# Warm-up matmuls on a preamble constant, an earlier gate for the wk load, and two matmuls ahead of Q, in a gated attention and feed-forward kernel

## The chip, the cores and the metric

The kernel runs on one core of a Trainium2 chip. The metric is the device time of one execution in microseconds (us). A core has five engines with instruction queues of their own: TensorE (PE, matrix products), VectorE (DVE), ScalarE (ACT), GpSimd (POOL) and SyncE (SP), which here issues transfers. Products of PE land in PSUM, from where VectorE and ScalarE copy them to SBUF, the working memory. Before the change the median of 8 runs is 267.02 us (266.33 to 267.93).

## The reference

```python
def _A_ref(x, wq, wk, wv, wo, beta):          # x: (1, 2048, 512), H = 32 heads of Dh = 16
    q, k, v = x @ wq, x @ wk, x @ wv          # as (B, H, N = 4 segments, L = 512, Dh)
    phi = lambda t: where(t > 0, t + 1, exp(t))
    M, z = 0, 0
    for s in range(4):
        p = softmax(qs @ ks.T * Dh ** -0.5 + causal_mask)
        a_dot = p @ vs
        a_mem = (phi(qs) @ M) / (phi(qs) @ z + 1e-6)
        outs.append(sigmoid(beta) * a_mem + (1 - sigmoid(beta)) * a_dot)
        M, z = M + phi(ks).T @ vs, z + phi(ks).sum(over the segment)
    return concat(outs) @ wo

def _B_ref(x, W_gate, W_up, W_down):          # F = 1792
    return (relu(x @ W_gate) * (x @ W_up)) @ W_down

g = sigmoid((A_x * gate_w).sum(-1))
return g * _A_ref(A_x, ...) + (1 - g) * _B_ref(A_x, ...)
```

## The kernel before

The sequence of 2048 rows is worked in four segments of 512. For each segment the kernel projects Q, K and V (matmuls of 128 x 128 against 512 columns, four to a result), forms the scores of 32 heads in 18 score products (`f`, L738, narrow matmuls of 32 rows), each followed by one exponential on ScalarE (L752, 1.9 us) and by causal masks on GpSimd (L760), and then the value products (`pv`, L849). Beside that run the gate and up products of the feed-forward part (`g` and `u`, 14 of each to a segment, L248), a ReLU on ScalarE, a product on VectorE, and the down and output products (`d` and `wo`). After each segment a state update (`mz`, L611) and reads of the state (`den`, `rec`) carry the memory M and z on. All dense matmuls are recorded at L248 by the helper `mm`; when the array is already laid out in column strips they are cut into four (L246).

The order of the work is not written by hand. The kernel records some 1350 operations with their engine, estimated cost, dependencies and buffers. A list scheduler (`Sched.run`) takes for each engine the operation that can start first, by keys, and emits all of them in that order. `MM` is the planned cost of a dense matmul, `SW` that of a change between PE's layouts (whole, rows, pairs, column strips); other costs stand in the calls of `op`. A change of a planned cost can thus change the order of all engines' instructions.

Four tiles G and one tile S in PSUM take PE's results. A G tile is used again only once its result has been copied out; S holds one score product at a time.

The start, which the change touches, goes as follows. The framework's preamble has GpSimd fill four small constant tiles, among them one of bfloat16 ones, and then releases all engines. `c_zero` has VectorE fill 128 x 128 ones in `zero`, a part of the output buffer `os` (L253). `c_dummy` (L291) runs 28 matmuls on `zero`, whose results nobody reads. `c_warm` (L263) runs one Exp on one column of `zero`, which loads ScalarE's table. SyncE and ScalarE each issue two quarters of the first segment's x, GpSimd issues wq in three pieces (L322). PE transposes x (`first_x`, L385) in groups of four matmuls, VectorE and ScalarE copy the transposes to xT (L393, L395), and PE forms Q for the first segment (L406) piece by piece of wq. K of the first segment follows, and needs wk.

The load of wk is tied to `o_wk0`, a memset of a single element of `wk_sb` on VectorE (L335). The planner puts it behind the first copy of xT. The transfer overwrites the element, so it has to wait for the memset, and SyncE, which issues in order, waits with wk and everything behind it: wv, gate_w, beta, and the pieces of W_gate and W_up.

Of the kernel before, what the change touches and what calls it, by code (L numbers as in the profile page):

```python
# [7 lines left out]
BF16 = mybir.dt.bfloat16  # L8
F32 = mybir.dt.float32
ACT = mybir.ActivationFunctionType  # L10
ALU = mybir.AluOpType

P = 128
# [12 lines left out]
VW = H * HP + 16  # L26
VSW = H // 2 * HP + 16

MM = 0.216
SW = 0.1  # L30
MG = 1.0


# [133 lines left out]
def kernel(  # L167
# [15 lines left out]
    nc = tc.nc  # L183
# [6 lines left out]
    def tl(name, shape, dt=BF16):  # L190
        return sb.tile(list(shape), dt, name=name)
# [11 lines left out]
    ident = tl("ident", [P, P])  # L203
    mcol = tl("mcol", [P, 1], F32)
    mcole = tl("mcole", [P, 1], F32)
    scratch = tl("scratch", [P, 1], F32)
    bdm = tl("bdm", [P, 8, DH], F32)
    mzacc = tl("mzacc", [P, NC, 2 * (DH + 1)], F32)
    M2 = [tl(f"M2_{i}", [P, NC, 8, DH]) for i in range(2)]
# [13 lines left out]
    Op_ = pool("O", 4, [P, 16, 2, DH])  # L223
    oTp = pool("oT", 8, [P, L])
    osp = rgp = pool("os", 4, [P, D])
    zero = osp.tiles[0]
    smp = pool("sm", 3, [P, 2, 16], F32)
    zg, zc, rcol, rp1, ngcol = (tl(n, [P, NT], F32) for n in ("zg", "zc", "rcol", "rp1", "ngcol"))
    R = [tl(f"R{s}", [P, 4, 4], F32) for s in range(NSEG)]
# [9 lines left out]
    op = sc.op  # L239
# [9 lines left out]
    ACTC = lambda n: 0.19 + 0.000833 * n  # L249


    def c_zero(e):
        nc.vector.memset(zero[:, 0:P], 1.0)  # L253
    o_zero = op("zero", {"DVE": 0.15}, c_zero, cls=0, key=-100)

    def c_ident(e):
        nc.gpsimd.memset(ident[:], 0.0)
# [2 lines left out]
    o_ident = op("ident", {"POOL": 0.6}, c_ident, cls=0, key=-100)  # L260

    def c_warm(e):
        nc.scalar.activation(scratch[:], zero[:, 0:1], ACT.Exp)  # L263
    o_warm = op("warm", {"ACT": 1.5}, c_warm, deps=[o_zero], cls=0, key=-100)

    def c_mcol(e):
# [20 lines left out]
    o_bdm = op("bdm", {"POOL": 1.5}, c_bdm, deps=[o_ident, o_vones], key=-10)  # L287

    def c_dummy(e):
        for _ in range(28):  # L290
            nc.tensor.matmul(g_dummy.t[:, 0:P], lhsT=zero[:, 0:P], rhs=zero[:, 0:P], start=True, stop=True)  # L291
    g_dummy = Buf(G)
    o_dummy = op("dummy", {"PE": 3.0}, c_dummy, deps=[o_zero], key=-1000, mode="D", alloc=[g_dummy])

# [18 lines left out]
    for i in range(2):  # L313
        for eng, q, h in (("SP", nc.sync, 0), ("ACT", nc.scalar, 1)):
            def f(e, i=i, q=q, h=h):
                q.dma_start(out=xn[0].t[:, 2 * h:2 * h + 2, 256 * i:256 * i + 256],
                            in_=x[256 * h:256 * h + 256, 256 * i:256 * i + 256].rearrange("(t p) d -> p t d", p=P))
# [14 lines left out]
        return load(name, f, P * tile_.shape[1] * (c1 - c0) * 2, key, eng=eng)  # L332

    lw["wk"] = loadw("wk", wk_sb, A_wk, 0, D, 1)
    o_wk0 = op("wk0", {"DVE": 0.08}, lambda e: nc.vector.memset(wk_sb[0:1, 0, 0:1], 0.0), key=-490, cls=0)  # L335
    lw["wk"].deps.append((o_wk0, None))
    lw["wv"] = loadw("wv", wv_sb, A_wv, 0, D, 1)

# [63 lines left out]
    first_x(1, None)  # L402
    for ci in range(NC):
        def f(e, ci=ci):
            for c in range(NC):
                nc.tensor.matmul(qS.t[:, c, :], lhsT=wq_sb[:, ci, c * P:(c + 1) * P], rhs=xT[0].t[:, ci, :],  # L406
                                 start=(ci == 0), stop=(ci == NC - 1))
        o_q0 = op(f"q0.{ci}", {"PE": 4 * MM * (1.5 if ci < 2 else 1)}, f,
                  deps=xc0[ci] + lwq[ci] + [(o_q0, 0.0) if ci else None],
                  key=-400 + ci, mode="D", alloc=[qS] + q0 if ci == 0 else [], uses=([] if ci == 0 else [qS]) + [xT[0]])  # L410
        if ci < 2:
            first_x(ci + 2, o_q0)
# [203 lines left out]
    def mz_deps(s):  # L616
        return [o_pKt[s, c] for c in range(NC)] + [o_v[s, t] for t in range(4)]
# [21 lines left out]
    def mz0():  # L639
        g = Buf(G)  # L640
        k = dkey(3)
        a = op("mz0", {"PE": 0.5}, lambda e: mz_mm(0, g), deps=mz_deps(0), key=k, mode="C", alloc=[g], uses=[pK[0], Vp[0]])
        mz_after(0, a, g, k)


# [74 lines left out]
    def unit(i):  # L720
        s, c = units[i]
        base = TA0 + (i // 2) * 2 * PU
        odd = i % 2
        FL = [[(c, 0, 0, 512)], [(c, 1, 0, 448), (c, 7, 448, 64)], [(c, 2, 0, 384), (c, 6, 384, 128)],
              [(c, 3, 0, 320), (c, 5, 320, 192)]]
        if not odd:
            FL.append([(c, 4, 0, 256), (c + 1, 4, 256, 256)])
        E, masks = {}, []
        for n, parts in enumerate(FL):
            sp, eb_ = Buf(Spool), Buf(Ep)  # L730
            kf = base + (n + 5 * odd) * 2 * PU / 9
            chunks = sorted({p[0] for p in parts})

            def f(e, parts=parts, sp=sp):
                for cc, kb, off, w in parts:
                    for j in range(4):
                        rows = slice(32 * j, 32 * j + 32)
                        nc.tensor.matmul(sp.t[:, j, off:off + w],  # L738
                                         lhsT=K2[s, cc].t[rows, kb, :, :].rearrange("p r k -> p (r k)"),
                                         rhs=QT[s, cc].t[rows, L - w:L], start=True, stop=True,  # L740
                                         tile_position=(32 * j, 0))
            a = op(f"f{s}{c}.{n}", {"PE": MM}, f,
                   deps=[o_q[s, cc] for cc in chunks] + [o for cc in chunks for o in o_k2[s, cc]] +
                   ([(fill_prev[0], 0.0)] if fill_prev[0] else []),
                   key=kf, mode="R", alloc=[sp], uses=[b_ for cc in chunks for b_ in (QT[s, cc], K2[s, cc])])
            fill_prev[0] = a
            if n == 1 and pending[0] is not None:
                rest(*pending[0], a)
                pending[0] = None

            def f(e, sp=sp, eb_=eb_):
                nc.scalar.activation(eb_.t[:], sp.t[:], ACT.Exp, scale=SCALE)  # L752
            b = op(f"e{s}{c}.{n}", {"ACT": 1.88}, f, deps=[a], key=kf, cls=0, alloc=[eb_], uses=[sp])
            offs = [p[2] for p in parts]

            def f(e, eb_=eb_, offs=offs):
                for off in offs:
                    for r in range(2):
                        v = eb_.t[64 * r:64 * r + 64, :, off:off + 64]
                        nc.gpsimd.affine_select(out=v, in_=v, compare_op=ALU.is_ge, fill=0.0, base=0,  # L760
                                                pattern=[[0, 4], [1, 64]], channel_multiplier=-1)
            m = op(f"m{s}{c}.{n}", {"POOL": 0.95 * len(parts)}, f, deps=[b], key=kf, uses=[eb_])
            for cc, kb, off, w in parts:
                if cc == c:
                    E[kb] = (eb_, off)
                else:
                    shared[s, cc] = (eb_, off, m)
            masks.append(m)
        if odd:
            E[4] = shared[s, c][0:2]  # L770
            masks.append(shared[s, c][2])
        pending[0] = (i, E, masks)
        if i == len(units) - 1:
            rest(i, E, masks, None)
# [4 lines left out]
    def dens(s, k0, org):  # L779
# [11 lines left out]
        rec_of[s, "den"] = rec_of[s, "mz"] = a  # L791
        if mds:
            gm = Buf(G)
            rec_of[s, "mz"] = am = op(f"mz{s}", {"PE": 0.5}, lambda e: mz_mm(s, gm), deps=[(a, 0.0)], key=k0 - 20, mode="C",
                                      alloc=[gm], uses=[pK[s], Vp[s]])
            gate_mz.append((s, am, gm, k0))
        T = Buf(Tp)
# [33 lines left out]
    def rest(i, E, masks, behind):  # L831
# [4 lines left out]
        def f(e):  # L836
            for kb in range(8):
                src, off = E[kb]
                w = L - 64 * kb
                for r in range(2):  # L840
                    rows = slice(64 * r, 64 * r + 64)
                    for j in range(4):
# [3 lines left out]
                        else:  # L846
# [1 line left out]
                            v = VS[s].t[rows, kb // 2, h * HP:h * HP + 32]  # L848
                        nc.tensor.matmul(gs[r].t[32 * j:32 * j + 32, L - w:L], lhsT=v, rhs=src.t[rows, j, off:off + w],  # L849
                                         start=(kb == 0), stop=(kb == 7), tile_position=(64 * r, 32 * j))  # L850
        a = op(f"pv{s}{c}", {"PE": 1.05}, f,
               deps=[(m, MG) for m in masks] + [o_v[s, t] for t in range(4)] + [o for t in range(4) for o in o_vs[s, t]] +
               ([(behind, 0.0)] if behind else []),
               key=k0 - 100, mode="P", alloc=gs, uses=list({id(v[0]): v[0] for v in E.values()}.values()) + [Vp[s], VS[s]])
# [170 lines left out]
```

The softmax here doesn't subtract the row's maximum and nothing guards it: scores larger than these inputs give would overflow.

## Time and profile before

| | us |
|---|---|
| median of 8 runs | 267.02 |
| profiled execution | 267.08 |
| its span, first to last instruction | 265.4 |
| PE busy | 260.5 (98%) |
| ScalarE busy | 194.1 (73%) |
| GpSimd busy | 191.3 (72%) |
| VectorE busy | 183.6 (69%) |
| wk, from issue to landing | 4.6 |

In a line of the timeline the first number is the start from the span's begin, the second the length, then follow engine, line of the kernel, operation, the tiles written and read, and the number of instructions that the line gathers. What stands in brackets is the engine's idle time just before, and what ended it. PEld is PE's weight load, SPq an issue of a transfer by SyncE. In a line of the chain of work, which is followed back from the last instruction, the time is that of a piece in which one engine went on without waiting. In the table of stretches the columns are the stretch, its length, the busy time of PE, PEld, DVE, ACT and POOL, PE's granted clock, the share of the DMA engines and GB/s. Matmuls overlap: the length of a group reaches to the modelled end of its last one, so distances are read from start to start.

### The profile page before, as it was taken

To read this page: it belongs to the slowest core of one execution; us is meant where nothing else is said; L and a number is where in the kernel's file an instruction comes from. 1 tells how busy PE (TensorE), PEld (TensorE's weight loads), DVE (VectorE), ACT (ScalarE), POOL (GpSimd) and SP (SyncE) were. 2 spreads that over 40 slices of the span, in tenths; PEclk is the share of its full clock that TensorE was granted. 3 is DMA by queue.
4 is the path that set the end of the run, shared out by engine and by line. 5 is a ranking of instruction groups with operands and counts; after the bars stand their busy time and mean duration, and the time that the engine had idled before them with its cause. 6 is when DMAs were issued, how large, how long until landed. Compare 5 with 4: busy or idle time off the path is not lost.

```text
span 265.4 us, 7084 instructions
## 1 busy us (share of the span) xinstructions
PE 260.5 (98%) x2844; PEld 115.0 (43%) x2844; DVE 183.6 (69%) x407; ACT 194.1 (73%) x189; POOL 191.3 (72%) x470
## 2 busy tenths in 40 slices
PE   8999999999999999999999999999999999999995
PEld 6434444444354434444444434344443444344444
DVE  1497888889975285998888837688985735566611
ACT  3598999899885558899896668898788566777010
POOL 8668888888559788798648988887878866537000
PEclk9999999999999999999999999999999999999999
DMA  5897990016310100000550010000000010000011
GB/s 161 248 266 198 337 268 15 4 40 69 111 26 1 42 20 22 0 2 2 117 110 16 21 42 20 4 2 0 2 0 4 0 42 23 20 2 0 2 41 40
DMA packets 27057, 15.54 MB, mean 59 GB/s; under 512 B 13584, under 2 KB 26896, under 8 KB 27024
## 3 DMA queue, kind: packets, MB, share of 16 engines
q1 hardware_dynamic: 26304, 14.30, 22.2%
q0 software_dynamic: 176, 0.52, 0.7%
q8 instruction: 22, 0.36, 0.6%
q10 hardware_dynamic: 544, 0.26, 0.3%
q14 instruction: 11, 0.09, 0.1%
HBM read 9.84 MB, written 2.10 MB: 45 GB/s over the span
## 4 chain that ended last, share of the span: by engine, by line
PE 96%; DMA 2%; DVE 0%; issue 0%; DVEq 0%
PE G L248 76%; PE S L738 9%; PE G L849 7%; PE G L246 3%; DMA wk_sb<-in_A_wk_dram 2%; PE G L291 1%; PE G L611 1%; PE G L785 0%; PE G L385 0%; DVE os L700 0%; DVE xT L393 0%; DVE os L253 0%; DVE mcole L268 0%; DVE wk_sb L335 0%; DVEq L700 0%
## 5 line engine op out<-in xcount | busy, mean ns | idle before, releaser
L752 ACT ACTIVATE E<-S 128x2048 bf16<-128x2048 f32 x72 | 135.1, 1876 | 34.5 <-PE S L738 32.1
L760 POOL TENSOR_SCALAR_AFFINE_SELECT E<-E 64x256 bf16<-64x256 bf16 x256 | 116.0, 453 | 38.1 <-ACT E L752 24.4
L248 PE MATMUL G<-xT,wu_sb 128*128 128x512 bf16 x218 | 58.3, 380 | 0.0
L248 PE MATMUL G<-xT,wg_sb 128*128 128x512 bf16 x218 | 57.9, 380 | 0.0
L663 DVE TENSOR_TENSOR hT<-G,os 128x512 bf16<-128x512 f32 x56 | 38.2, 684 | 20.2 <-ACT os L659 10.8
L248 PE MATMUL G<-wd_sb,hT 128*128 128x512 bf16 (+1 forms) x222 | 50.7, 366 | 0.0
L884 DVE STREAM_TRANSPOSE T<-G 128x512 f32<-128x512 f32 x44 | 30.3, 702 | 14.0 <-PE G L849 8.3
L659 ACT ACTIVATE os<-G 128x512 bf16<-128x512 f32 x56 | 32.7, 597 | 6.1 <-PE G L248 5.3
L248 PEld LDWEIGHTS <-wu_sb 128*128 128x128 bf16 x218 | 19.9, 98 | 24.8 <-issue 3.0
L248 PEld LDWEIGHTS <-wg_sb 128*128 128x128 bf16 x218 | 19.4, 98 | 24.6 <-issue 4.1
L248 PEld LDWEIGHTS <-hT 128*128 128x128 bf16 x222 | 20.3, 98 | 22.3 <-issue 2.6
L738 PE MATMUL S<-QT,K 32*128 32x192 bf16 (+7 forms) x512 | 28.5, 287 | 0.0
L738 PEld LDWEIGHTS <-K 32*128 32x128 bf16 x512 | 8.2, 92 | 30.3 <-issue 29.9
L700 DVE TENSOR_SCALAR os<-G,ngcol 128x512 bf16<-128x512 f32 (+1 forms) x10 | 7.0, 696 | 19.3 <-PE G L248 19.2
L849 PE MATMUL G<-E,Vp 64*32 64x128 bf16 (+7 forms) x512 | 19.0, 284 | 0.1
L849 PE MATMUL G<-E,VS 64*32 64x128 bf16 (+7 forms) x512 | 18.4, 284 | 0.0
L248 PE MATMUL G<-wo_sb,oT 128*128 128x512 bf16 (+1 forms) x68 | 17.6, 367 | 0.0
L597 POOL COPY VS<-Vp 64x256 bf16<-64x256 bf16 x32 | 13.3, 417 | 4.9 <-DVE Vp L515 3.5
L248 PE MATMUL G<-xT,wk_sb 128*128 128x512 bf16 x62 | 16.0, 380 | 0.5 <-DMA wk_sb<-in_A_wk_dram 0.5
L702 ACT ACTIVATE os<-G,ngcol 128x512 bf16<-128x512 f32 x7 | 4.8, 687 | 15.0 <-PE G L248 15.0
L904 DVE TENSOR_TENSOR O<-T,sm 128x256 bf16<-128x256 f32 x32 | 15.6, 516 | 0.3
L479 POOL COPY R<-rcol 32x4 f32<-32x4 f32 x64 | 13.5, 211 | 3.0
(98 smaller groups left out, 300.7 us busy)
## 6 DMA issues: line engine op xcount, KB each, us to landing
out_dram<-os SPq DMA_DIRECT2D x15, 128.0 KB, 1.7
wd_sb<-in_B_W_down_dram SPq DMA_DIRECT2D x1, 1792.0 KB, 12.6
xn<-in_A_x_dram SPq DMA_DIRECT2D x3, 512.0 KB, 4.7
wg_sb<-in_B_W_gate_dram SPq DMA_DIRECT2D x2, 512.0 KB, 5.9
wu_sb<-in_B_W_up_dram SPq DMA_DIRECT2D x2, 512.0 KB, 7.0
wg_sb<-in_B_W_gate_dram SPq DMA_DIRECT2D x3, 256.0 KB, 6.6
wu_sb<-in_B_W_up_dram SPq DMA_DIRECT2D x3, 256.0 KB, 6.9
wk_sb<-in_A_wk_dram SPq DMA_DIRECT2D x1, 512.0 KB, 4.6
```

Of the source, the lines that this page charges most:

```text
L246: nc.tensor.matmul(out_ap[q], lhsT=lhsT[:, q], rhs=rhs, start=start, stop=stop, tile_position=(0, 32 * j))
L248: nc.tensor.matmul(out_ap, lhsT=lhsT, rhs=rhs, start=start, stop=stop)
L479: nc.gpsimd.tensor_copy(R[s][32 * j:32 * j + 32, k, :], rcol[32 * k:32 * k + 32, cols])
L597: nc.gpsimd.tensor_copy(VS[s].t[64 * r:64 * r + 64, t, 0:H // 2 * HP].rearrange("p (h v) -> p h v", v=HP)[:, :, 0:DH], src[:, :, r, 0:DH])
L659: nc.scalar.activation(rg.t[:], g.t[:], ACT.Relu)
L663: nc.vector.tensor_tensor(h.t[:], u.t[:], rg.t[:], ALU.mult)
L738: nc.tensor.matmul(sp.t[:, j, off:off + w], lhsT=K2[s, cc].t[rows, kb, :, :].rearrange("p r k -> p (r k)"), rhs=QT[s, cc].t[rows, L - w:L] ...
L752: nc.scalar.activation(eb_.t[:], sp.t[:], ACT.Exp, scale=SCALE)
L760: nc.gpsimd.affine_select(out=v, in_=v, compare_op=ALU.is_ge, fill=0.0, base=0, pattern=[[0, 4], [1, 64]], channel_multiplier=-1)
L849: nc.tensor.matmul(gs[r].t[32 * j:32 * j + 32, L - w:L], lhsT=v, rhs=src.t[rows, j, off:off + w], start=(kb == 0), stop=(kb == 7), tile_po ...
L884: nc.vector.transpose(T.t[:].rearrange("p b e -> p (b e)"), g.t[:])
L904: nc.vector.tensor_tensor(O.t[:, :, r, :], T.t[:, :, 0:DH], sm.t[:, r, :, None].to_broadcast([P, 16, DH]), ALU.mult)
```

## The change

The ones tile and its memset go. Warm-up matmuls and the Exp read the preamble's constant of ones, broadcast along the columns. There are 31 warm-up matmuls instead of 28. The Exp writes its result into the first column of `wk_sb`, and the memset of `wk_sb` becomes an empty operation, so that the transfer of wk is ordered behind the Exp. The planner still sees `zero` and `wk0` with their former costs. Two matmuls of ones are put ahead of Q's first four, into S, which these overwrite. Beside that, planned costs are changed: `MM` 0.216 to 0.2159, `SW` 0.1 to 0.094, score products `MM` to 0.229, value products 1.05 to 1.015, state updates 0.5 to 0.56. With them the planner's order differs from near the first segment's end on.

```diff
-MM = 0.216
-SW = 0.1
+MM = 0.2159
+SW = 0.094
...
-    scratch = tl("scratch", [P, 1], F32)
...
-    zero = osp.tiles[0]
...
-    def c_zero(e):
-        nc.vector.memset(zero[:, 0:P], 1.0)
-    o_zero = op("zero", {"DVE": 0.15}, c_zero, cls=0, key=-100)
+    ones = nc.const_aps.tensor(1.0, [P, P], BF16)
+    o_zero = op("zero", {"DVE": 0.15}, lambda e: None, cls=0, key=-100)
...
     def c_warm(e):
-        nc.scalar.activation(scratch[:], zero[:, 0:1], ACT.Exp)
+        nc.scalar.activation(wk_sb[:, 0, 0:1], ones[:, 0:1], ACT.Exp)
...
     def c_dummy(e):
-        for _ in range(28):
-            nc.tensor.matmul(g_dummy.t[:, 0:P], lhsT=zero[:, 0:P], rhs=zero[:, 0:P], start=True, stop=True)
+        for _ in range(31):
+            nc.tensor.matmul(g_dummy.t[:, 0:P], lhsT=ones, rhs=ones, start=True, stop=True)
...
-    o_wk0 = op("wk0", {"DVE": 0.08}, lambda e: nc.vector.memset(wk_sb[0:1, 0, 0:1], 0.0), key=-490, cls=0)
+    o_wk0 = op("wk0", {"DVE": 0.08}, lambda e: None, key=-490, cls=0)
     lw["wk"].deps.append((o_wk0, None))
...
         def f(e, ci=ci):
+            if ci == 0:
+                for _ in range(2):
+                    nc.tensor.matmul(qS.t[:, 0, 0:P], lhsT=ones, rhs=ones, start=True, stop=True)
             for c in range(NC):
                 nc.tensor.matmul(qS.t[:, c, :], lhsT=wq_sb[:, ci, c * P:(c + 1) * P], rhs=xT[0].t[:, ci, :],
                                  start=(ci == 0), stop=(ci == NC - 1))
...
-        a = op("mz0", {"PE": 0.5}, lambda e: mz_mm(0, g), deps=mz_deps(0), key=k, mode="C", alloc=[g], uses=[pK[0], Vp[0]])
+        a = op("mz0", {"PE": 0.56}, lambda e: mz_mm(0, g), deps=mz_deps(0), key=k, mode="C", alloc=[g], uses=[pK[0], Vp[0]])
...
-            a = op(f"f{s}{c}.{n}", {"PE": MM}, f,
+            a = op(f"f{s}{c}.{n}", {"PE": 0.229}, f,
...
-            rec_of[s, "mz"] = am = op(f"mz{s}", {"PE": 0.5}, lambda e: mz_mm(s, gm), deps=[(a, 0.0)], key=k0 - 20, mode="C",
+            rec_of[s, "mz"] = am = op(f"mz{s}", {"PE": 0.56}, lambda e: mz_mm(s, gm), deps=[(a, 0.0)], key=k0 - 20, mode="C",
...
-        a = op(f"pv{s}{c}", {"PE": 1.05}, f,
+        a = op(f"pv{s}{c}", {"PE": 1.015}, f,
```

## The prediction

> **What bounds the kernel now.** I read the page's busy shares first, then its chain of waits.
>
> ```profile
> span 265.4 us, 7084 instructions
> ...
> PE 260.5 (98%) x2844; PEld 115.0 (43%) x2844; DVE 183.6 (69%) x407; ACT 194.1 (73%) x189; POOL 191.3 (72%) x470
> ...
> PE 96%; DMA 2%; DVE 0%; issue 0%; DVEq 0%
> ```
>
> TensorE (PE) is the chain for 96% of the span. So only three things can move the time: work on PE, gaps between its matmuls, and the tail after the last one. The one DMA in the chain is wk, 2% of the span. Next I read the timeline of the first 16 us.
>
> ```profile
> 0.89 0.17 DVE L253 MEMSET os<- 128x128 bf16 x1 [0.89 <-PEq L1009]
> ...
> 1.12 3.17 PE L291 MATMUL G<-os 128*128 128x128 bf16 x28 [1.12 <-DVE mcole L268]
> ...
> 3.15 0.20 ACT L263 ACTIVATE scratch<-os 128x1 f32<-128x1 bf16 x1
> ...
> 4.08 1.06 PE L385 MATMUL G<-ident,xn 128*128 128x128 bf16 x8
> ...
> 5.19 1.23 PE L406 MATMUL S<-xT,wq_sb 128*128 128x512 bf16 x4
> 5.20 0.06 DVE L335 MEMSET wk_sb<- 1x1 bf16 x1
> 5.31 0.37 SPq L331 DMA_DIRECT2D wk_sb<-in_A_wk_dram  x1
> ...
> 9.93 2.76 PE L248 MATMUL G<-xT,wk_sb 128*128 128x512 bf16 x12 [0.47 <-DMA wk_sb<-in_A_wk_dram]
> ...
> 13.91 0.10 PEld L738 LDWEIGHTS <-K 32*128 32x128 bf16 x4 [0.42 <-DVE K L561]
> ```
>
> SyncE issues wk's transfer at 5.31, just behind VectorE's one-element memset of wk_sb, which ends at 5.26. PE wants wk when Q is through and waits for it until 9.93. The other gaps I looked for in a table of stretches:
>
> ```profile
> 9.46:9.93 0.47, 0.00 (x1) 0.01 (x1) 0.00 (x0) 0.44 (x1) 0.47 (x1) 1.00 1.09 383
> 9.93:13.92 3.99, 3.99 (x19) 1.68 (x21) 3.03 (x7) 2.99 (x6) 1.27 (x6) 1.00 0.85 218
> 13.92:44.90 30.98, 30.98 (x337) 12.98 (x336) 26.29 (x66) 28.16 (x32) 26.08 (x71) 1.00 0.93 225
> 44.90:46.40 1.50, 1.38 (x73) 0.84 (x66) 1.10 (x4) 1.50 (x2) 1.27 (x4) 1.00 0.00 0
> 46.40:262.00 215.60, 215.60 (x2367) 93.71 (x2366) 151.03 (x316) 157.94 (x145) 154.01 (x378) 1.00 0.11 26
> ```
>
> The second and third figures are the stretch's length and PE's busy time. From 9.93 to 262 PE is never idle but for 0.12 us near 45. There a value product (pv of segment 0, chunk 1) waits for GpSimd's masks, and takes 1.41 us from its first matmul to the next operation's, where its like takes 1.11: a stall of 0.30. So the kernel has two gaps worth a name: wk, and that 0.30.
>
> **The change, part by part.** The profiled execution took 267.08 us, 265.4 of them span and 1.68 around it. The median of the runs is 267.02, so the sum is made on the profiled one and carried over 0.06 lower.
>
> *wk.* The Exp that loads ScalarE's table now writes one column of wk_sb, and the transfer waits for that write instead of the memset. The row above ends at 3.35, and from VectorE's memset to SyncE's issue took 0.05, so wk is issued at about 3.40, 1.9 earlier. It took 4.57 from issue to landing (9.88), so with nothing else on the DMA engines it lands near 8.0. The wait of VectorE's memset for the first copy of xT goes with it. Behind wk on SyncE's queue stand wv, gate_w, beta and the first W_gate and W_up pieces. They wait for transfers that landed by 4.7, and move up too. Nothing of SyncE is held back, since it had nothing else to do between 1.77 and 5.31.
>
> What does PE get? Q's last matmul starts at 9.08 and the next at 9.93, where the usual distance is 0.216: 0.63 us. Not all of it is kept. The first score matmuls (13.92) need a K tile that VectorE finishes at 13.29, and VectorE and ScalarE work towards it from Q's end at 9.46 without regard to when wk comes: four Q evacuations, each behind the other, from 9.49 to 12.17, then the copies of K and the masks on it. The K tile is thus ready for PE at about 13.35, 0.57 before PE uses it. With wk early that product waits next, for 0.06. Gain 0.57.
>
> *Warm-up.* Without the memset PE waits only for the release at the start. VectorE went from its release (0.75) to its first instruction in 0.15; PE's release ends at 0.78, so I put its start at 0.92, between 0.85 and 1.0. The 28 matmuls stand 0.1067 apart, so 31 take 3.31, and the transposes begin at about 4.23, 0.15 later than now. The x they wait for landed at 3.88, so nothing but the warm-up holds them. The copies of xT shift by 0.15 with them, and so does Q's first matmul, to 5.33.
>
> Against this stands the clock. Its record rises to full at 5.65, 4.53 after PE's start; the 128-column matmuls stand 0.107 apart before and 0.056 after. Q's first four take 1.07 instead of 0.86, so 0.21 is lost to the slow clock. Were the rise tied to PE's start, it would come at 5.45 and Q would lose only 0.06: Q's end then stays where it is. Were it fixed in time, Q would lose 0.16 and end 0.10 late. I take 0, between −0.15 (transposes in part at full clock) and +0.10.
>
> The Trainium skill, page "TensorE: Matmul & The Clock Gate", section "Part 1: The HAM clock gate", says that the rise follows a free-running window of 3.4 us, so that it need not follow an earlier start, and varies by half a microsecond between runs. This trace shows one rise only, and cannot confirm it; by the rule, as my estimate, the warm-up would be worth anything from −0.25 to +0.25.
>
> *Fillers.* Two matmuls of 0.107 after the first eight transposes, 5.08 to 5.30, while PE waits for xT and wq until 5.33. They cost nothing while that wait covers them, and 0.21 if it were gone. They write a part of S that Q then overwrites.
>
> *wq beside wk.* wq's packets fill the DMA engines from 3.8 to 5.8. wk's first packet went out 0.9 after issue, so now it comes at about 4.3, in the middle of them. The three wq pieces landed at 5.08, 5.67 and 6.69 and are used at 5.19, 6.48 and 7.57. The last has 0.88 to spare. At best nothing changes; at worst all of wk's 512 KB goes first, at the 75 KB per 0.2 us that the trace shows, 1.4 us, and Q waits 0.5. The slack is nearer to a shared delay of half of that (0.7), so I take 0.
>
> The page "DMA: Bandwidth & Descriptors", section "Queues, rings and completion order", speaks against this: an engine takes turns between queues, packet by packet, so wk would slow wq. With turns even in bytes, my estimate from it is a delay of some 0.7 to 1.0 and a wait of at most 0.1.
>
> *The order.* New planner costs move PE's order from the 117th of its 584 operations on, near 50 us. Compared in the two builds: 72 score products, 16 value products, three state updates, 12 reads in both; 170 changes of tile layout before, 171 after; 34 dense matmuls cut into four column strips before, 12 after. Prices come from the chain:
>
> ```profile
> 14.31 2.70 PE G L248 x12
> 17.34 2.70 PE G L248 x12
> ...
> 78.13 2.60 PE G L246 x48
> ```
>
> Twelve dense matmuls take 12 times 0.216 = 2.59, so a score product with both its changes of layout is 3.03 − 2.59 = 0.44, of which its own matmuls take 0.33 and the changes 0.11. Strips (48 for 12) cost no more than whole matmuls: 0 to 0.2 over 22 of them. The one more change is +0.1. So the moved order is worth +0.1, and its real risk is new waits. The shortest distances that PE leaves others shrink in places: 1.42 us, three times, between a gate product and the next that uses its bank (1.52 once before). ReLU there takes 0.60 and the hand-overs some 0.25, so it holds while ScalarE comes at once; 1.39 held in the trace of before. I take no new wait, between 0 and +1.3. The 0.30 near 45 stays, as it lies before the reordering, or goes.
>
> Sum: −0.57 + 0 + 0 + 0.1 = −0.47; 267.02 − 0.47 is about 266.5. A difference of 0.2%, 0.53 us, is about what a measurement of this kernel can tell from none, so the forecast lies on that edge.
>
> **The rivals.** *A new wait in the moved order (slower).* A score exponential takes 1.88 on ScalarE. Where one starts just ahead of a ReLU that PE's bank waits for, the bank is free 0.25 + 1.88 + 0.60 = 2.7 after the product, and PE, which left 1.42, waits 1.3. The places are the gate products 3 and 7 of segment 2 and 0 of segment 3. One such place gives 267.02 − 0.47 + 1.3 = 267.85. It turns the sign once it costs more than 0.47 and counts as slower from 1.0. For it: ScalarE is 73% busy, and the 0.30 near 45 shows that plans are missed. Against it: in all three places the new order on ScalarE has the ReLU ahead of that exponential.
>
> *wq late behind wk (no difference).* Q waits up to 0.5 for its third piece, and what wk gave is gone: 267.0. It decides once that piece lands after 7.57. For it: DMA is full from 4 to 5.6. Against: 0.88 of slack.
>
> *Clock early and the stall gone (faster than forecast).* The rise comes before Q and the 0.30 near 45 goes: −0.15 − 0.30 more, 266.05. For it: PE starts 0.2 earlier and has no hole before Q. Against: nothing in the masks' order ahead of 45 changes.
>
> **How the numbers follow.** Forecast 0.52 (266.2 to 266.8), more gain 0.16, wq late 0.15, new wait 0.17. Of the forecast's half, 0.30 lies below the edge at 266.49 and 0.22 above it, as the Q of more runs than the profiled one may meet an earlier clock. So faster is 0.30 + 0.16 = 0.46, same 0.22 + 0.15 = 0.37, slower 0.17. The range reaches from 266.0, which takes in the case of more gain but for its end, to 267.6, which takes in wq late and the smaller new waits.
>
> **What would show it.** PE's first matmul near 0.9; wk issued near 3.40 and landed before 9.3; no PE gap ahead of the first K matmul; the first score matmuls near 13.35 instead of 13.92; the clock's rise at 5.45 or earlier; no new PE gap after 50. It would be wrong if wq's third piece landed after 7.57, if Q ended later than 9.5, or if PE waited for ScalarE or a bank in segments 1 to 3.

## The result: slower by half a percent, and the profile after

The changed kernel takes 268.40 us in the median of 11 runs (267.59 to 269.28), the one before 266.98 in the median of 32 (266.33 to 267.93). The ratio is 1.0055, with a 95% interval of 1.0042 to 1.0067: slower by 1.42 us. The forecast was 266.5, with a range that ended at 267.6, and mostly for faster. It was wrong in sign and size.

The profiled execution took 268.40, of which 266.7 are span and 1.7 lie around it. So in this pair of executions all of the loss lies in the span (265.4 before). The page, its first lines and its chain:

```profile
span 266.7 us, 6972 instructions
...
PE 261.1 (98%) x2783; PEld 115.5 (43%) x2783; DVE 180.6 (68%) x401; ACT 196.6 (74%) x193; POOL 190.3 (71%) x470
...
PE 95%; DMA 2%; POOL 1%; DVE 0%; issue 0%; POOLq 0%; DVEq 0%
PE G L246 77%; PE S L738 9%; PE G L849 7%; DMA wq_sb<-in_A_wq_dram 2%; PE G L244 1%; PE S L406 1%; PE G L611 1%; POOL wq_sb L319 0%; PE G L785 0%; DVE hT L663 0%; DVE os L700 0%; POOL ident L255 0%; POOL ident L254 0%; POOLq L255 0%; DVEq L700 0%
```

The changed kernel's file is two lines shorter ahead of the helper `mm`: its dense matmuls stand at L246, and those cut into column strips at L244. The shares hardly differ from those of before. What tells is the name of the one DMA in the chain: it was wk, and is now wq. The timeline of the first 16 us shows the place:

```profile
0.83 3.46 PE L288 MATMUL G<-const-bfloat16-1.0 128*128 128x128 bf16 x31 [0.83 <-PEq L1009]
...
3.15 0.20 ACT L260 ACTIVATE wk_sb<-const-bfloat16-1.0 128x1 bf16<-128x1 bf16 x1
3.38 0.37 SPq L328 DMA_DIRECT2D wk_sb<-in_A_wk_dram  x1
...
4.09 1.06 PE L382 MATMUL G<-ident,xn 128*128 128x128 bf16 x8
...
4.95 0.42 PE L404 MATMUL S<-const-bfloat16-1.0 128*128 128x128 bf16 x2
...
5.20 1.14 PE L406 MATMUL S<-xT,wq_sb 128*128 128x512 bf16 x4
...
9.15 1.90 PE L406 MATMUL S<-xT,wq_sb 128*128 128x512 bf16 x8 [1.50 <-DMA wq_sb<-in_A_wq_dram]
...
10.88 2.75 PE L246 MATMUL G<-xT,wk_sb 128*128 128x512 bf16 x12
...
14.94 0.10 PEld L738 LDWEIGHTS <-K 32*128 32x128 bf16 x4 [0.50 <-DVE K L561]
```

wk is let go at 3.38, as intended. But Q stops for 1.50 us ahead of its third part, for wq's third piece, and starts it at 9.15 (7.57 before). That piece, issued at 3.18 in both kernels, landed at 6.69 before and at 9.10 now. K then follows without a gap, but from 10.88 (9.93 before), and the first score matmuls start at 14.94 (13.92 before), 1.02 later. wk itself landed at 9.86, against 9.88 before: 1.92 earlier on its way, and not a bit earlier there. From the first score matmuls to the end the two executions differ by 0.29; that is no more than the kernel before differs from itself there (248.9, 248.7 and 249.1 in its three executions). 0.24 us of it stands behind one wait of VectorE near 139 us for a transfer. Five of the experiments' profiles have that wait too, with 0.24 to 0.41 lost on PE, three of them with the old order, so it doesn't belong to the new one. 1.02 and 0.29 are the 1.31 by which the spans differ.

The traffic of the queues in two stretches of 1 us (packets, MB, share of the 16 engines' time; q0 is GpSimd's queue with wq, q1 SyncE's) shows what happened to wq. Before, from 4.4 to 5.4:

```profile
DMA packets 95, 0.27 MB, mean 270 GB/s; under 512 B 29, under 2 KB 29, under 8 KB 95
...
q0 software_dynamic: 95, 0.27, 97.8%
```

After, from 4.4 to 5.4:

```profile
DMA packets 43, 0.08 MB, mean 83 GB/s; under 512 B 7, under 2 KB 28, under 8 KB 43
...
q0 software_dynamic: 22, 0.06, 50.8%
q1 hardware_dynamic: 21, 0.02, 19.1%
```

After, from 5.4 to 6.4:

```profile
q1 hardware_dynamic: 275, 0.28, 84.6%
q0 software_dynamic: 18, 0.03, 10.8%
```

After, from 6.4 to 7.4:

```profile
q0 software_dynamic: 57, 0.20, 59.9%
q1 hardware_dynamic: 166, 0.17, 47.5%
```

In the first microsecond in which wk's packets go out, hardly anything moves, on either queue: 0.08 MB where wq alone had moved 0.27. In the second wk takes nine parts of ten. Only in the third do the two share about evenly, and then 0.20 MB of wq are still to go. The engines weren't idle in the first: there wq's 22 packets took 50.8% of the 16 engines' time, 0.37 us each, where 95 packets took 97.8% before, 0.16 us each.

The slow first microsecond is wk's own, and the trace of before has it too. There wk starts when wq is through, and from 6.4 to 7.4 its queue, alone, moves no more than this:

```profile
DMA packets 83, 0.08 MB, mean 85 GB/s; under 512 B 0, under 2 KB 83, under 8 KB 83
...
q1 hardware_dynamic: 83, 0.08, 75.3%
```

The change has laid this start on top of wq.

### The profile page after: what moved, and what is told of

Same layout as the page of the kernel before. It is cut to its first block, busy times and chain, and to the rows that moved or that the text cites. A ratio compares the mean times of both kernels' runs of the same rounds, so it can differ in the third digit from the quotient of the medians.

```text
span 266.7 us, 6972 instructions
## 1 busy us (share of the span) xinstructions
PE 261.1 (98%) x2783; PEld 115.5 (43%) x2783; DVE 180.6 (68%) x401; ACT 196.6 (74%) x193; POOL 190.3 (71%) x470
## 4 chain that ended last, share of the span: by engine, by line
PE 95%; DMA 2%; POOL 1%; DVE 0%; issue 0%; POOLq 0%; DVEq 0%
PE G L246 77%; PE S L738 9%; PE G L849 7%; DMA wq_sb<-in_A_wq_dram 2%; PE G L244 1%; PE S L406 1%; PE G L611 1%; POOL wq_sb L319 0%; PE G L785 0%; DVE hT L663 0%; DVE os L700 0%; POOL ident L255 0%; POOL ident L254 0%; POOLq L255 0%; DVEq L700 0%
## 5 line engine op out<-in xcount | busy, mean ns | idle before, releaser
L246 PE MATMUL G<-xT,wu_sb 128*128 128x512 bf16 x224 | 59.6, 380 | 0.1
L246 PE MATMUL G<-xT,wg_sb 128*128 128x512 bf16 x224 | 59.7, 380 | 0.0
L246 PE MATMUL G<-wd_sb,hT 128*128 128x512 bf16 (+1 forms) x232 | 53.0, 367 | 0.0
L246 PEld LDWEIGHTS <-wu_sb 128*128 128x128 bf16 x224 | 20.4, 98 | 25.8 <-issue 3.8
L246 PEld LDWEIGHTS <-hT 128*128 128x128 bf16 x232 | 21.2, 98 | 23.4 <-issue 2.8
L246 PEld LDWEIGHTS <-wg_sb 128*128 128x128 bf16 x224 | 20.0, 98 | 25.5 <-issue 4.3
L700 DVE TENSOR_SCALAR os<-G,ngcol 128x512 bf16<-128x512 f32 (+1 forms) x9 | 6.2, 686 | 18.8 <-PE G L246 18.8
L246 PE MATMUL G<-wo_sb,oT 128*128 128x512 bf16 (+1 forms) x68 | 17.8, 367 | 0.0
L702 ACT ACTIVATE os<-G,ngcol 128x512 bf16<-128x512 f32 x8 | 5.5, 687 | 15.9 <-PE G L246 15.9
L926 POOL TENSOR_TENSOR O<-O,O 128x512 bf16<-128x512 bf16 x11 | 13.0, 1185 | 4.2 <-DVE O L904 3.6
L246 PE MATMUL G<-xT,wk_sb 128*128 128x512 bf16 x62 | 15.9, 380 | 0.0
```

Source lines behind the costliest of these rows:

```text
L246: nc.tensor.matmul(out_ap, lhsT=lhsT, rhs=rhs, start=start, stop=stop)
L700: nc.vector.tensor_scalar(ob.t[:, cs], g.t[:, 0:W], ngcol[:, tt:tt + 1], None, ALU.mult)
L926: (nc.vector if e == "DVE" else nc.gpsimd).tensor_tensor(Oa.t[:], Oa.t[:], Ob.t[:], ALU.add)
```

## The experiments

All are compared with the kernel before on the same chip, whose median was 266.79 beside the first four, 266.85 beside the next four, then 266.87, and 267.11 beside the last. Its median span was 265.1 or 265.2 in the first three groups, and the time outside the span is 1.7 to 1.8 in each of its runs.

**The gate: undone, and alone**

```diff
 # k1_gate_back, against the changed kernel
-        nc.scalar.activation(wk_sb[:, 0, 0:1], ones[:, 0:1], ACT.Exp)
+        nc.scalar.activation(scratch[:], ones[:, 0:1], ACT.Exp)
...
-    o_wk0 = op("wk0", {"DVE": 0.08}, lambda e: None, key=-490, cls=0)
+    o_wk0 = op("wk0", {"DVE": 0.08}, lambda e: nc.vector.memset(wk_sb[0:1, 0, 0:1], 0.0), key=-490, cls=0)
 # k2_gate_alone, against the kernel before
-        nc.scalar.activation(scratch[:], zero[:, 0:1], ACT.Exp)
+        nc.scalar.activation(wk_sb[:, 0, 0:1], zero[:, 0:1], ACT.Exp)
...
-    o_wk0 = op("wk0", {"DVE": 0.08}, lambda e: nc.vector.memset(wk_sb[0:1, 0, 0:1], 0.0), key=-490, cls=0)
+    o_wk0 = op("wk0", {"DVE": 0.08}, lambda e: None, key=-490, cls=0)
```

> The changed kernel with wk's old gate: the memset of one element of wk_sb behind the first copies of xT is back, the Exp writes a scratch column; warm-up on the constant, the two matmuls ahead of Q and the new order stay. Theory (wk and wv, let go at 3.4, take turns on the DMA engines with wq, and Q waits for wq's last piece): that piece lands near 6.7 instead of 9.1, wk near 9.9, PE's gap of 1.5 ahead of Q's third part goes and the 0.47 ahead of K comes back; 266.9 to 267.3. Rival one (the moved order of the work costs most of the 1.4): stays at 268.0 or more. Rival two (31 warm-up matmuls and the two more hold Q back): stays at 268.0 or more, and Q's third part starts later than 7.7.

> The kernel before with wk's gate alone changed: its Exp writes the first column of wk_sb, the memset of wk_sb is gone; warm-up from the memset of ones, 28 matmuls, old order. Theory of the turns: wq's last piece lands near 9.1, Q's third part starts near 9.15, the first score matmuls near 14.9; 267.0 + 1.0 = 268.0 (267.7 to 268.3). Rivals one and two: no loss from the gate, 266.4 to 267.0.

With the old gate put back, the rest of the change takes 266.99, ratio 1.0008 [0.9992, 1.0023]: no difference from before. wq's third piece landed at 6.57, Q's parts started at 5.20, 6.50 and 7.59 with no wait, and wk, issued at 5.32, landed at 9.27. There PE did not wait for wk either: the 0.47 ahead of K that was expected back did not come. The gate alone, on the kernel before, takes 267.55, ratio 1.0026 [1.0016, 1.0036]; its median span is 265.8. The timeline of its start has the same stop:

```profile
3.38 0.37 SPq L331 DMA_DIRECT2D wk_sb<-in_A_wk_dram  x1
...
8.60 1.90 PE L406 MATMUL S<-xT,wq_sb 128*128 128x512 bf16 x8 [1.08 <-DMA wq_sb<-in_A_wq_dram]
```

wq's third piece landed at 8.55. So the early gate is enough to make the kernel slower, and without it the change isn't slower. But 0.7 us in the span is only half of the loss, and 267.55 lies below the 267.7 to 268.3 that was expected.

**The order undone**

```diff
 # k3_old_order, against the changed kernel: the planned costs of before
-MM = 0.2159
-SW = 0.094
+MM = 0.216
+SW = 0.1
...
-        a = op("mz0", {"PE": 0.56}, lambda e: mz_mm(0, g), deps=mz_deps(0), key=k, mode="C", alloc=[g], uses=[pK[0], Vp[0]])
+        a = op("mz0", {"PE": 0.5}, lambda e: mz_mm(0, g), deps=mz_deps(0), key=k, mode="C", alloc=[g], uses=[pK[0], Vp[0]])
...
-            rec_of[s, "mz"] = am = op(f"mz{s}", {"PE": 0.56}, lambda e: mz_mm(s, gm), deps=[(a, 0.0)], key=k0 - 20, mode="C",
+            rec_of[s, "mz"] = am = op(f"mz{s}", {"PE": 0.5}, lambda e: mz_mm(s, gm), deps=[(a, 0.0)], key=k0 - 20, mode="C",
...
-            a = op(f"f{s}{c}.{n}", {"PE": 0.229}, f,
+            a = op(f"f{s}{c}.{n}", {"PE": MM}, f,
...
-        a = op(f"pv{s}{c}", {"PE": 1.015}, f,
+        a = op(f"pv{s}{c}", {"PE": 1.05}, f,
```

> The changed kernel with the planned costs of before, so that PE's order is that of before, and all else as changed. Theory of the turns: the gap ahead of Q's third part stays at 1.5; the order takes with it 0.1 of layout changes and the new wait of 0.24 near 139 us; 268.0 to 268.2. Rival one (order): 267.0 or less. Rival two (warm-up): 268.4.

It takes 267.82, ratio 1.0039 [1.0024, 1.0053]: 0.4 us less than the changed kernel, when each is taken against the kernel before beside it (+1.03 and +1.42). The median spans are 266.1 and 266.15, so inside the span the order is worth nothing that shows. The difference lies outside it. In all 7 runs of this kernel the time outside the span is 1.7 to 1.8; of the 12 runs of the changed kernel whose span is on record (the 11 above and one of 267.46) four have 2.7 to 2.9. I come back to these below. One thing in the span stays open: this kernel, with the early gate and the new warm-up, is 1.0 longer than the one before, the early gate alone 0.7, and the warm-up alone (below) 0.15. No run says where the rest comes from.

**wq's third piece out of the way, by SyncE and by ScalarE**

```diff
 # k4_wq3_sync, against the changed kernel (k7_old_order_wq3_sync: the same, with the planned costs of before)
-            nc.gpsimd.dma_start(out=wq_sb[:, c0:c1, :], in_=A_wq[c0 * P:c1 * P, :].rearrange("(c p) n -> p c n", p=P))
+            (nc.sync if c0 == 2 else nc.gpsimd).dma_start(out=wq_sb[:, c0:c1, :], in_=A_wq[c0 * P:c1 * P, :].rearrange("(c p) n -> p c n", p=P))
 # k12_wq3_act: nc.scalar in the place of nc.sync
```

> The changed kernel with one edit: the third piece of wq (256 KB) is issued by SyncE, ahead of wk in the same queue, instead of by GpSimd. Theory of the turns between queues: within a queue wk can't overtake it, so the piece lands before 7.3, Q runs through to about 9.2, and if wk lands by then the first score matmuls start near 13.4 to 13.9; 266.6 to 267.2. If it is not the turns but the DMA engines being short of rate as a whole once wk starts, the piece or wk is late anyway: 267.6 or more.

> The changed start (warm-up on the constant, two matmuls ahead of Q, wk behind the Exp) with the old planned costs, and wq's third piece issued by SyncE ahead of wk. If the turns of the queues and the late fetch of the program are all that was lost: no gap ahead of Q's third part, 1.7 outside the span, and what the early wk gives shows: 266.3 to 266.6. If wk early gives nothing in most runs, because wk lands before Q's end in them anyway: 266.7 to 266.9, the same as before.

> The changed kernel, but wq's third piece is issued by ScalarE just behind its Exp, so that its transfer and wk's start from two hardware queues at the same moment, near 3.4. The question is whether the third piece is late because it stands on GpSimd's queue, or because any queue beside wk's is. Theory A (GpSimd's queue is the one that is passed over): between two hardware queues the turns are about even in packets, the 256 KB of the piece go out together with the first 256 KB of wk, and it lands between 6.5 and 7.6, before PE wants it or at most 0.3 late; the first score matmuls start between 13.3 and 13.9. Theory B (SyncE's queue with wk and wv behind it takes nearly all, whatever stands beside it): the piece lands at 8.0 or later as before, PE waits 0.5 or more for it, and the first score matmuls start at 14.1 or later.

The first gives 266.90, ratio 1.0001 [0.9988, 1.0014], against 268.40 for the changed kernel: with the third piece ahead of wk in wk's own queue, all of the loss is gone. The timeline of its start:

```profile
3.38 0.37 SPq L328 DMA_DIRECT2D wk_sb<-in_A_wk_dram  x1
...
5.14 1.04 PE L406 MATMUL S<-xT,wq_sb 128*128 128x512 bf16 x4 [0.43 <-DMA wq_sb<-in_A_wq_dram]
...
6.50 0.55 PEld L406 LDWEIGHTS <-wq_sb 128*128 128x128 bf16 x4 [0.27 <-DMA wq_sb<-in_A_wq_dram]
...
7.60 1.89 PE L406 MATMUL S<-xT,wq_sb 128*128 128x512 bf16 x8
...
9.33 2.75 PE L246 MATMUL G<-xT,wk_sb 128*128 128x512 bf16 x12
...
13.38 0.39 PE L738 MATMUL S<-QT,K 32*128 32x512 bf16 x4
```

The piece landed at 6.74, wk at 8.23, and the first score matmuls start at 13.38: the path that the prediction described, to 0.03 us. In the stretch from 4.4 to 5.4 its queues moved 0.30 MB, so the slow microsecond is not there. That the start agrees so closely is in part chance: in this execution the clock rose early, at 3.85, and what that gave was lost again, as PE waited for wq's first piece and then for the second, which landed at 6.46 (5.67 before). With the old order as well it takes 267.06, ratio 1.0005 [0.9993, 1.0017], and the first score matmuls start at 13.39, with the clock's rise at 5.69. So the early gate without its harm gives no gain, in either order. That the forecast gain is missing needed an answer of its own (below).

The third, with the piece on ScalarE's queue, takes 267.05, ratio 0.9998 [0.9983, 1.0013]; the piece landed at 6.75 and the first score matmuls start at 13.52. The time agrees with "GpSimd's queue is the one passed over", but the premise failed: ScalarE's sequencer issued the transfer at 1.92, while the Exp ahead of it ran only at 3.15, so it didn't start beside wk. It doesn't decide that question. GpSimd's second piece, which it ran beside, landed at 6.60 (5.67 before) and held up Q's second part by 0.18. Whether a late piece on a hardware queue would be passed over too stays open.

**wk alone early, wv and what follows held**

```diff
 # k5_wv_held, against the changed kernel
-    o_wk0 = op("wk0", {"DVE": 0.08}, lambda e: None, key=-490, cls=0)
+    o_wk0 = op("wk0", {"DVE": 0.08}, lambda e: nc.vector.memset(wv_sb[0:1, 0, 0:1], 0.0), key=-490, cls=0)
```

> The changed kernel with wk let go behind the Exp as there, but wv and everything behind it held as before: the memset of one element, behind the first copies of xT, now writes wv_sb. It tells whether wk alone or wk and wv together hold wq's last piece back. If wk's 512 KB alone take turns with it: the piece lands near 7.5 to 8.2 instead of 8.6 to 9.1, and the span is between 265.2 and 265.8. If any transfer on SyncE's queue does it to the full, whatever its length: 8.6 to 9.1 as in the changed kernel, span 266.1. If it is wv and what follows: before 7.2, span 265.1.

It takes 267.41, ratio 1.0020 [1.0008, 1.0032], span 265.7. wv is issued at 4.89 instead of 3.79, which is still before wq's third piece is through. wq's third piece landed at 8.16, and Q's third part waits 0.66:

```profile
8.20 1.90 PE L406 MATMUL S<-xT,wq_sb 128*128 128x512 bf16 x8 [0.66 <-DMA wq_sb<-in_A_wq_dram]
```

So wk, with wv 1.1 later, delays wq by about 1.5 us, more than the slack. wv right behind it may add to that; but between one execution and the next the landing varies too much (8.16 to 9.10 over the five kernels that have the early gate and no cure) to measure its share from single profiles.

**A shorter instruction stream**

```diff
 # k6_wide_warm, against the changed kernel
-        for _ in range(31):
-            nc.tensor.matmul(g_dummy.t[:, 0:P], lhsT=ones, rhs=ones, start=True, stop=True)
+        wide = nc.const_aps.tensor(1.0, [P, L], BF16)
+        for _ in range(8):
+            nc.tensor.matmul(g_dummy.t[:], lhsT=ones, rhs=wide, start=True, stop=True)
```

> The changed kernel with 8 warm-up matmuls of 512 columns in place of 31 of 128: the same 3.4 us of PE, but 46 fewer instructions in PE's program. In the changed kernel the last block of PE's program is fetched at 261.4, 1.8 before PE's last matmul, and 4 of 12 runs have 2.7 us or more outside the span instead of 1.7. If that late fetch is what makes the time outside the span longer, the fetch falls away or its place moves past the end, all runs have 1.7 to 1.9 outside, and the median is near 267.9 with a span of 266.1 as before. If the time outside has another cause: again some runs with 2.7, median 268.4.

The warm-up lasts as long, with 46 PE instructions fewer. It takes 267.39, ratio 1.0021 [1.0009, 1.0033], and the time outside the span is 1.7 to 1.8 in all 12 runs. This goes with the loading of the program. The queue q8, named "instruction" in the profile, brings blocks of 16 KB. Its last block started at 248 to 250 in every profile with the old order, and at 248 here. In the profiles of the changed kernel's order with 31 short matmuls it started at 259.9 to 266.4. In three of these (259.9 to 261.4) the time outside was 1.7. In the other two the block came after the last instruction: with wq's piece on SyncE (at 266.4, span 264.9, 267.07 in all, so 2.2 outside) and on ScalarE (at 266.3, span 265.2, 267.14 in all, 1.9 outside). The traffic of the first from 266 to 268:

```profile
core 0 of [0], span 264.9 us
...
DMA packets 1, 0.02 MB, mean 8 GB/s; under 512 B 0, under 2 KB 0, under 8 KB 0
...
q8 instruction: 1, 0.02, 3.0%
```

Counted over the runs: with the new order and 31 short matmuls, 9 of 56 had 2.2 or more outside the span (4 of 12 of the changed kernel, 1 of 12 with the gate put back, 2 of 12 and 2 of 8 with the third piece on SyncE and on ScalarE, 0 of 12 with wv held). With the old order or the wide warm-up it was none of 75, and none of the 97 runs of the kernel before beside them. That a late block goes with a long time outside is seen in those two profiles; for the runs of 2.2 and more without a profile it is argued from the counts. Over the 12 runs of the changed kernel it makes the mean time outside 2.09 instead of 1.7. The median span of the kernel with the wide warm-up is 0.45 below the changed kernel's; in its profile Q waits 0.74 instead of 1.50. Whether the wide warm-up has a part in that is open.

**The warm-up alone**

```diff
 # k8_warm_alone, against the kernel before: no ones tile, 31 warm-up matmuls and the Exp on the constant, two matmuls ahead of Q; old gate, old order
-        nc.vector.memset(zero[:, 0:P], 1.0)
...
-        for _ in range(28):
-            nc.tensor.matmul(g_dummy.t[:, 0:P], lhsT=zero[:, 0:P], rhs=zero[:, 0:P], start=True, stop=True)
+        for _ in range(31):
+            nc.tensor.matmul(g_dummy.t[:, 0:P], lhsT=ones, rhs=ones, start=True, stop=True)
...
+            if ci == 0:
+                for _ in range(2):
+                    nc.tensor.matmul(qS.t[:, 0, 0:P], lhsT=ones, rhs=ones, start=True, stop=True)
```

> The kernel before with the warm-up alone changed: 31 matmuls on the constant without a memset, two more ahead of Q, old gate of wk, old order. Forecast of the warm-up was 0, between 0.15 less and 0.10 more: 266.7 to 266.9 beside 266.8. If the warm-up costs: 267.0 or more.

266.99, ratio 1.0000 [0.9988, 1.0013]. The warm-up and the fillers are worth nothing that shows, as forecast. In its profile the clock's record rose at 3.95 and the first score matmuls started at 12.96; its median span is 265.25 all the same.

**The kernel before, again**

> The kernel before, unchanged, for a second profiled execution. The question is why neither kernel in which wq's third piece is safe and wk comes early (first score matmuls at 13.38 and 13.39) is faster than the one before, whose profiled execution started them at 13.92. Theory A (that execution was one with a late wk): wk, issued near 5.3, lands anywhere from 8.8 to 9.9, as it did in the two kernels with the old gate (issued 5.32 and landed 9.27; issued 4.91 and landed 8.83); here it lands before 9.6, PE waits less than 0.3 for it, and the first score matmuls start between 13.3 and 13.7. Theory B (the 13.92 is the rule, and the kernels with the early wk lose 0.5 later on): wk lands near 9.9 again, the first score matmuls start at 13.8 to 14.0, and the span from there to the end is 251.4 to 251.5 as before.

> The kernel before once more, a third profiled execution, with the same expectations as the second: by theory A wk's landing differs between these executions by 0.3 or more and the start of the first score matmuls follows it down to a floor near 13.35; by theory B both lie within 0.15 of 9.88 and 13.92.

Unchanged, it gave 266.94 (ratio 1.0003 [0.9989, 1.0018]) and, in a single run, 267.01. The two timelines, first and second:

```profile
5.30 0.37 SPq L331 DMA_DIRECT2D wk_sb<-in_A_wk_dram  x1
...
9.34 2.76 PE L248 MATMUL G<-xT,wk_sb 128*128 128x512 bf16 x12
...
13.33 0.40 PE L738 MATMUL S<-QT,K 32*128 32x512 bf16 x4
```

```profile
5.30 0.37 SPq L331 DMA_DIRECT2D wk_sb<-in_A_wk_dram  x1
...
9.59 2.75 PE L248 MATMUL G<-xT,wk_sb 128*128 128x512 bf16 x12
...
13.64 0.39 PE L738 MATMUL S<-QT,K 32*128 32x512 bf16 x4
```

wk landed at 9.30 and 9.32, not at 9.88, and the first score matmuls start at 13.33 and 13.64. In the second PE doesn't wait for wk at all: there the clock rose at 6.25 and Q itself was later. So in three executions of the same kernel the first score matmuls start at 13.92, 13.33 and 13.64. The gap that the prediction wanted to win was that of a single execution.

**Both cures together**

```diff
 # k11_wide_wq3_sync, against the changed kernel
-        for _ in range(31):
-            nc.tensor.matmul(g_dummy.t[:, 0:P], lhsT=ones, rhs=ones, start=True, stop=True)
+        wide = nc.const_aps.tensor(1.0, [P, L], BF16)
+        for _ in range(8):
+            nc.tensor.matmul(g_dummy.t[:], lhsT=ones, rhs=wide, start=True, stop=True)
...
-            nc.gpsimd.dma_start(out=wq_sb[:, c0:c1, :], in_=A_wq[c0 * P:c1 * P, :].rearrange("(c p) n -> p c n", p=P))
+            (nc.sync if c0 == 2 else nc.gpsimd).dma_start(out=wq_sb[:, c0:c1, :], in_=A_wq[c0 * P:c1 * P, :].rearrange("(c p) n -> p c n", p=P))
```

> The changed kernel with both mends: wq's third piece issued by SyncE ahead of wk, and the warm-up as 8 matmuls of 512 columns instead of 31 of 128, which takes 46 instructions from PE's queue. If the late program fetch is set by the place of an instruction block near the end, the last fetch comes near 248, the time outside the span is 1.7 to 1.8 in all runs (with the third piece on SyncE alone 2 of 12 had 2.2 and 2.7), and the time is 266.7 to 267.0, ratio 0.999 to 1.001: the same as before, since the early wk is worth at most some tenths. If the early wk is worth its 0.57 and the late fetch hid it, ratio 0.998 or less.

266.58 in the median of 12, ratio 0.9991 [0.9980, 1.0003]. The time outside the span is 1.7 to 1.8 in all runs, and the last block started at 248.3. It is faster than the changed kernel by 1.7 us, each taken against the kernel before beside it, and can't be told from the kernel before. Its profiled execution was its slowest run (267.55): the clock rose at 6.17, and wk landed only at 10.13, so that PE waited 0.40 for it, although wq's third piece had landed at 6.04. Why wk came so late there is open.

## Why the prediction was wrong

*The step that failed is "wq beside wk".* It was taken as 0, with Q waiting 0.5 at worst. The third piece's landing was delayed by 2.4 us, not by 0.7, and Q's third part came 1.58 later. The mechanism was named, also as the rival "wq late behind wk", and so was the sign that would show it (a landing after 7.57). The size was wrong because of its bound: "all of wk's 512 KB goes first, at the 75 KB per 0.2 us" supposes that the two queues together run at the rate that one had alone. In the microsecond after wk's first packets they moved 0.08 MB together. The trace of before had the half of it, wk's slow start from 6.4 to 7.4 (shown above); I took only the full rate that followed. Whoever lays that start over wq has to ask what wq does meanwhile, and at worst it does nothing: with that microsecond counted, the bound would have been 2.4 instead of 1.4, and a wait of 1.5. That this meets the profile of the changed kernel is in part chance: over the five kernels with the early gate and no cure the piece was late by 1.5 to 2.4. The rival's time of 267.0 was too low for the same reason. The slower rival that stood in the prediction, a ReLU kept waiting in the moved order, was not what happened: 1.02 of the span's 1.31 is there before the moved order begins (near 56, not near 50 as the prediction has it), and taking the order back leaves the span as it is. Two figures of the prediction were misread, without weight for the outcome: wk's first packet went out 1.04 after its issue (at 6.34), not 0.9, and 1.16 after it in the changed kernel (at 4.55); and the rival "clock early and the stall gone" adds up to 266.10, not 266.05.

*The page cited there.* The Trainium skill, "DMA: Bandwidth & Descriptors", section "Queues, rings and completion order", has an engine take turns between queues at packet boundaries. It spoke against the change and was right in direction. Turns even in bytes, as I took them, are what the third microsecond shows (0.20 and 0.17 MB). In the second it was 0.03 to 0.28, in the first nearly nothing for either, so the wait of at most 0.1 that I estimated from it was far too small.

*wk, −0.57.* With wq's third piece in SyncE's queue the path is as described in two profiles of three: no gap ahead of K, first score matmuls at 13.38 and 13.39 against 13.35 worked out. But two terms fail. As the change was made, wk landed no earlier (9.86), so "lands near 8.0" held only with nothing else on the engines, as that sentence itself said; with the third piece on SyncE it was 7.8 and 8.2, and 10.13 in the kernel with both cures. And 0.57 was measured against one execution. The three starts of before, 13.33, 13.64 and 13.92, leave −0.05 to 0.54, in the mean 0.25, and the cured kernels, in either order, show no gain beyond their intervals. In the five profiles with the old gate the distance from Q's last matmul to K's first, less the usual 0.216, is 0.63, 0.26 and three times nothing: in most of them wk was there in time without the early gate. And where the clock rose at nearly the same moment, the first score matmuls of the old gate came no later than those of a cured kernel: 12.96 (warm-up alone, rise at 3.95) beside 13.38 (3.85), 13.37 (gate put back, 5.66) beside 13.39 (5.69), 13.64 (kernel before, 6.25) beside 14.17 (both cures, 6.17). Only the execution that the prediction was read from, 13.92 with the rise at 5.65, is an exception.

*Warm-up and fillers, 0.* Right: 1.0000 for these alone, with an interval of some 0.3 us either way. PE started at 0.83 (0.92 forecast) and the transposes at 4.09 (4.23 forecast). The clock did not follow PE's start: the rise came at 4.81, 5.65 and 6.25 in three executions of the kernel before, with PE's first matmul at 1.11 to 1.12 in each. The page "TensorE: Matmul & The Clock Gate", "Part 1: The HAM clock gate", says so of its free-running window; the spread here, 1.4 us over three, is more than the half microsecond either way that it gives.

*The order, +0.1.* Nothing speaks against it inside the span: 266.15 against 266.1, though 0.1 is too little to be told. What wasn't foreseen is the block of program at the end, outside the span. It was not among the steps at all, since the sum dealt with the span and took the 1.68 around it as fixed.

*Where the 1.42 went, in all:* the changed kernel's median span is 266.15. The kernel before has 265.1 to 265.2 in the first three groups of experiments, so the span grew by about 1.0, and the cure on SyncE takes back 0.95 of that. The mean time outside the span grew by 0.39 (2.09 less 1.70). Together that is about 1.4.

## What to carry to other kernels

Before a transfer is let go earlier, list the transfers that are still under way then and the slack of each. Price their delay by how the queues behaved where two of them already met, not by the full rate shared out: here 0.9 us of slack was not enough against a transfer of 512 KB started beside the last 256 KB of another queue, while putting the urgent piece ahead in the same queue cost nothing that the time shows. A gap at the start that is read in one profiled execution should be seen in two or three before it is counted as a gain.

## What the runs showed of the hardware that was not expected

- wk's transfer starts slowly where SyncE's queue had nothing under way ahead of it: alone, it moved 0.08 to 0.12 MB in the microsecond after its first full packet (five profiles with the late gate), and 0.29 to 0.38 MB in the next. Beside it wq moved 0.02 to 0.05 MB in that microsecond in all five kernels with the early gate and no cure, and 0.00 to 0.03 MB in the half microsecond after it, against 0.14 to 0.18 MB of SyncE's queue. With the 256 KB of wq ahead in the same queue there was no such microsecond (0.30 to 0.36 MB from 4.4 to 5.4 in three profiles). Why it is so is open.
- The time outside the span is not fixed. In the order whose last 16 KB block of program came after 259 in each of five profiles, 9 of 56 runs had 2.2 to 2.9 us outside instead of 1.7; in the profile with 2.2 the block came after the last instruction. With 46 instructions fewer on PE it came at 248, and no run was long.
- Unchanged, the kernel's first score matmuls start anywhere from 13.33 to 13.92, as the clock's rise (4.81 to 6.25) and wk's landing (9.30 to 9.88) vary; its span varies from 264.3 to 266.1.
- ScalarE's sequencer issued a transfer 1.2 us before the Exp ahead of it in its program ran.
